# The second batch's keys and queries: transposed by VectorE in 32 by 32 blocks and placed by transfers

## The chip, the cores and the metric

The kernel runs on one core of a Trainium2 chip. The core has five engines with an instruction stream each: TensorE (PE in the profile; its weight loads are PEld), VectorE (DVE), ScalarE (ACT), GpSimd (POOL) and SyncE (SP), which here only issues transfers. TensorE writes to eight banks of PSUM; everything else lies in SBUF, in 128 partitions. The metric is the device time of one execution in microseconds (us), as the median of several runs. Beside it, one execution was recorded by the hardware profiler; all durations of single instructions come from that one.

## What is computed

Windowed attention with a few global tokens, and behind it a two-layer network on all its outputs. There are 8 batches and 8 heads, 512 local and 32 global tokens, head size 64; the model width is 512 and the hidden width 2048. Everything is in 32-bit floats.

```python
scale = 1.0 / np.sqrt(D)
k_all = np.concatenate([k_g, k_l], axis=2)
v_all = np.concatenate([v_g, v_l], axis=2)
out_g = np.matmul(sm(scale * np.matmul(q_g, k_all.transpose(0, 1, 3, 2))), v_all)
s_ll = scale * np.matmul(q_l, k_l.transpose(0, 1, 3, 2))
mask = np.abs(pos[:, None] - pos[None, :]) <= window          # window = 32
s_ll = np.where(mask, s_ll, -1000000000.0)
s_lg = scale * np.matmul(q_l, k_g.transpose(0, 1, 3, 2))
out_l = np.matmul(sm(np.concatenate([s_lg, s_ll], axis=-1)), v_all)
attn_out = np.concatenate([out_g, out_l], axis=2)
x = attn_out.transpose(0, 2, 1, 3).reshape(B * S, H * D)      # 4352 rows of 512
h = x @ w_in
y = (h - np.tanh(h)) @ w_out
```

`sm` is the softmax. The scores of one local token against local keys matter only within 32 places on either side, so a tile of 128 queries needs 192 local keys and the 32 global ones.

## The kernel before

**Tiling.** A head's 512 local tokens are four tiles of 128. Both factors of a score, queries and keys, must lie with the head size of 64 in the partitions. In memory they lie with the tokens outermost, so each head's keys and queries have to be transposed. The keys are then laid out in a buffer of four windows of 224 columns (192 local keys, 32 global ones, line 417 and following).

**Three ways of the attention.** The first two batches (heads 0 to 15) are worked in plain 32-bit floats and in pairs of heads (class `Pair`, eight pairs, pairs 4 to 7 are the second batch): head 2j lies in partitions 0 to 63, head 2j+1 in 64 to 127. `Pair.add_load` (472) loads both heads' keys and queries with the tokens in partitions; `Pair.add_turn` (484) transposes them by TensorE, four 128 by 128 transposes into one bank for the keys and four into another for the queries (line 493), and copies them from the banks to the key windows `first_kw` and to `first_q` (line 324, called from 499 to 504). The first batch has two sets of buffers in turn. The second batch has one set, the third of `SETS` (262): raw tile `rawkq`, key windows `kw0`, queries `hk0`. Batches 2 to 7 are worked head by head with each factor split in a high and a low part; their keys and queries go another way, `add_transposed` (678): loaded in 32 by 32 blocks, transposed block by block by VectorE (691), split, and moved to their windows by transfers (`Head.add_turn`, 780).

**The rest of a head.** Local scores (617, or 879 and 880) go to banks; VectorE masks them and finds the peak (884), ScalarE takes the exponential (891), VectorE the inverse of the sum (627, or 898), GpSimd scales (904), TensorE transposes the probabilities (972, or 1055 among the products of the head before) and multiplies them with the values (649, 1053). The global queries' scores have lines 526 and 827.

**Feed-forward.** A batch's output of 512 tokens is one chunk. Its 16 steps multiply with a block of `w_in` (1136, or 1162 for the first steps of the first chunk), take `h - tanh(h)` (1144, 1147), split it (324, 1153) and multiply with a block of `w_out` into four banks (1199). Each product is made of three passes of high and low parts. The feed-forward work of one batch is spread between the attention of the next. During the first two batches the weights are loaded too, in 32 pieces (377), and split.

**What sets the order.** Every step is recorded by `add` with an engine (or a choice of engines), an estimated duration, a due time and the buffers that it reads and writes. `Order.run` (109) then walks through all steps and emits, again and again, the one that could start first by these estimates, due times deciding between near equals. So the order on each engine, SP's queue among them, is fixed when the program is built, and each engine works strictly in that order. The due times come from a table of numbers, `CFG` (302). `mode` marks kinds of TensorE work; a switch between kinds is given an estimated cost. Only one tile holds the raw and the transposed blocks of the later batches: `raw1` and `kq` are the two halves of `rawkq` (213).

## Time and profile before

| | before |
|---|---|
| median of 3 runs | 1014.32 us (1011.75 to 1015.07) |
| the profiled execution | 1015.1 us, its span 1013.3 us |
| instructions in it | 18,583 |
| granted TensorE clock, mean | 0.999 |
| moved by transfers | 91.66 MB, 90 GB/s on average |

The span is the stretch from the first to the last recorded instruction; 1.8 us of the execution lie outside it. Busy time is the union of an engine's instructions; matmuls overlap their neighbours, so how long a group holds TensorE is read from one start to the next. A releaser ("<-") names what ended an idle time.

### The profile page before, as it was taken

The numbers are of one execution on the slowest core, as the hardware profiler recorded it, in microseconds if no ns is written. First come the engines' busy times: TensorE is split into PE (matmuls) and PEld (weight loads), VectorE is DVE, ScalarE is ACT, GpSimd is POOL, SyncE is SP. The second block draws the span as 40 slices with busy tenths as digits, with TensorE's granted clock in tenths as the row PEclk, the third lists the DMA queues.
The fourth block names the chain that finished last, engine by engine and source line by source line (L and its number), as shares of the span: only waits on it lengthen the run. The fifth ranks groups of instructions, "written<-read, shape, count | busy, mean of one in ns | idle before, by whom it ended". The sixth has DMA issues, their size and how long they took to land.

```text
span 1013.3 us, 18583 instructions
## 1 busy us (share of the span) xinstructions
PE 991.5 (98%) x5648; PEld 826.4 (82%) x5648; DVE 605.8 (60%) x1826; ACT 669.2 (66%) x1783; POOL 613.5 (61%) x839
## 2 busy tenths in 40 slices
PE   6999999999999999999999999999999999999998
PEld 4677777888888888888888888888887888888897
DVE  6965665787668665777558674777657774111110
ACT  5966666886778766878568775877658775422231
POOL 4665556676767765777567765777657774322221
PEclk9999999999999999999999999999999999999999
DMA  9555454443454333543344432643245330100010
GB/s 233 144 152 162 123 149 111 124 93 81 84 124 98 81 76 80 125 86 85 74 106 111 89 84 52 146 91 85 56 93 129 80 88 15 42 1 1 1 42 21
DMA packets 250819, 91.66 MB, mean 90 GB/s; under 512 B 204640, under 2 KB 238176, under 8 KB 250720
## 3 DMA queue, kind: packets, MB, share of 16 engines
q1 hardware_dynamic: 248928, 89.82, 37.9%
q8 instruction: 45, 0.74, 0.3%
q10 hardware_dynamic: 1792, 0.66, 0.2%
q14 instruction: 54, 0.44, 0.1%
HBM read 49.27 MB, written 8.91 MB: 57 GB/s over the span
## 4 chain that ended last, share of the span: by engine, by line
PE 84%; DVE 5%; ACT 2%; DMA 1%; issue 1%; SPq 1%; POOL 1%; ACTq 0%; DVEq 0%; POOLq 0%
PE bank L1199 34%; PE bank L1136 32%; PE bank L1053 5%; PE bank L1055 4%; PE bank L879 2%; PE bank L880 2%; DVE stats L898 1%; DVE prob L884 1%; DVE pg L839 1%; PE bank L827 1%; PE bank L649 1%; PE bank L972 1%; DVE tlo L989 1%; PE bank L617 1%; DMA wraw<-in_moe_w_in_dram 1%
## 5 line engine op out<-in xcount | busy, mean ns | idle before, releaser
L1199 PE MATMUL bank<-w_out_hi,gates 128*128 128x512 f32 x1088 | 302.1, 395 | 0.2
L1153 POOL TENSOR_TENSOR gates<-t,gates 128x512 fp32r<-128x512 f32 x136 | 175.5, 1290 | 171.5 <-PE bank L1199 124.0
L1199 PEld LDWEIGHTS bank<-w_out_hi,gates 128*128 128x128 f32 x1088 | 198.7, 188 | 42.4 <-POOL gates L1153 2.3
L1147 DVE TENSOR_TENSOR t<-bank,t 128x512 f32<-128x512 f32 x136 | 94.0, 691 | 178.2 <-ACT t L1144 176.3
L1144 ACT ACTIVATE t<-bank 128x512 f32<-128x512 f32 x136 | 81.3, 598 | 127.5 <-PE bank L1136 119.3
L1199 PE MATMUL bank<-w_out_lo,gates 128*128 128x512 f32 x544 | 152.2, 393 | 0.0
L1136 PE MATMUL bank<-x_hi,w_in_hi 128*128 128x512 f32 x496 | 137.5, 399 | 0.0
L904 POOL TENSOR_SCALAR prob<-prob,stats 128x224 f32<-128x224 f32 x240 | 106.4, 459 | 45.4 <-DVE stats L899 14.1
L1136 PE MATMUL bank<-x_lo,w_in_hi 128*128 128x512 f32 x496 | 133.7, 391 | 0.0
L1136 PE MATMUL bank<-x_hi,w_in_lo 128*128 128x512 f32 x496 | 133.6, 391 | 0.0
L324 ACT CAST gates<-t 128x512 fp32r<-128x512 f32 x136 | 84.1, 618 | 58.8 <-PE bank L1199 43.8
L891 ACT ACTIVATE prob<-prob,stats 128x224 f32<-128x224 f32 x240 | 113.3, 474 | 10.2 <-DVE stats L884 8.2
L1199 PEld LDWEIGHTS bank<-w_out_lo,gates 128*128 128x128 f32 x544 | 100.8, 188 | 20.1
L884 DVE CUSTOM_DVE_ANT_0 prob<-bank,mask 128x224 f32<-128x224 f32 x240 | 80.9, 388 | 55.4 <-PE bank L880 45.4
L1136 PEld LDWEIGHTS bank<-x_hi,w_in_lo 128*128 128x128 f32 x496 | 91.6, 188 | 19.0 <-issue 0.5
L1136 PEld LDWEIGHTS bank<-x_lo,w_in_hi 128*128 128x128 f32 x496 | 91.2, 188 | 18.2
L324 ACT COPY wraw<-bank 64x288 f32<-64x288 f32 (+1 forms) x130 | 57.8, 446 | 69.8 <-PE bank L1053 48.4
L1136 PEld LDWEIGHTS bank<-x_hi,w_in_hi 128*128 128x128 f32 x496 | 87.9, 189 | 15.0 <-issue 0.2
L1053 PE MATMUL bank<-thi,vv 128*128 128x160 f32 (+2 forms) x384 | 96.8, 294 | 1.6 <-DVE stats L839 1.6
L1055 PE MATMUL bank<-idr,prob 128*128 128x128 f32 x376 | 98.0, 280 | 0.1
L1088 POOL TENSOR_TENSOR x_lo<-wraw,x_hi 64x256 fp32r<-64x256 f32 x96 | 70.6, 735 | 39.7 <-ACT x_hi L324 32.7
L1053 PE MATMUL bank<-tlo,vv 128*64 128x160 f32 (+2 forms) x384 | 89.4, 234 | 0.0
(144 smaller groups left out, 1785.1 us busy)
## 6 DMA issues: line engine op xcount, KB each, us to landing
hl<-hl SPq DMA_DIRECT2D x72, 128.0 KB, 2.3
out_dram<-wraw SPq DMA_DIRECT2D x32, 256.0 KB, 2.4
kw<-hl SPq DMA_DIRECT2D x72, 96.0 KB, 2.2
wraw<-in_moe_w_in_dram SPq DMA_DIRECT2D x12, 512.0 KB, 3.8
rawkq<-in_k_l_dram SPq DMA_DIRECT2D x96, 64.0 KB, 2.3
rawkq<-in_q_l_dram SPq DMA_DIRECT2D x96, 64.0 KB, 2.4
vraw<-in_v_l_dram SPq DMA_DIRECT2D x48, 128.0 KB, 2.4
kw<-hl SPq DMA_DIRECT2D x72, 80.0 KB, 2.1
```

What stands on the lines that cost most here:

```text
L324: (nc.scalar.copy if e == "A" else nc.vector.tensor_copy)(dst, src)
L884: nc.vector.tensor_tensor_reduce(out=self.tile(t)[:, :KC], in0=getattr(self, f"s_{pair}")[:, i, :KC], in1=tile_mask[t], scale=-0.125, scal ...
L891: nc.scalar.activation(x, x, AF.Exp, bias=self.st[:, t:t + 1], scale=-1.0, accum_out=self.st[:, 4 + t:5 + t])
L904: nc.gpsimd.tensor_scalar(x, x, self.st[:, 8 + t:9 + t], 1.0, op0=ALU.mult, op1=ALU.mult)
L1053: nc.tensor.matmul(dst, l, r, start=i == 0, stop=i == len(mm) - 1, skip_group_check=True)
L1055: nc.tensor.transpose(*turns[i // each], idn)
L1088: eng[e].tensor_sub(places()[1], view(total, [(160, 2), (1, P)]), f32(places()[0]))
L1136: nc.tensor.matmul(self.h[s][:, j * n:(j + 1) * n], w[:, cc, f * P:(f + 1) * P], self.x()[xi][:, cc, :n], start=part == 0 and cc == 0 and ...
L1144: nc.scalar.activation(tt_[q], self.h[s], AF.Tanh)
L1147: nc.vector.tensor_sub(tt_[q], self.h.pop(s), tt_[q])
L1153: eng[e].tensor_sub(gg[q][1], tt_[q].rearrange("p (k c) -> p k c", k=4), f32(gg[q][0]))
L1199: nc.tensor.matmul(self.acc[tt], g[:, j * nt + tt], low_out(f) if wi else w_out_hi[:, f], start=s == 0 and k == 1, stop=last and k == 3 * ...
```

## The change

Pairs 4 to 7, the second batch, no longer go through TensorE. For each head, four transfers load keys and queries in blocks of 32 by 32 into `raw1` (128-byte pieces, 512 to a transfer, where a transfer had 512 pieces of 256 bytes before); one VectorE instruction transposes all blocks into `kq`, which puts the keys in partitions 0 to 63 and the queries in 64 to 127; two transfers place the keys in their windows and one the queries. Head 1 of a pair goes the same way through the same tiles after head 0. The scores of a pair now also wait for the second head's keys and queries (`self.more`). The copies of the global keys stay.

The planner changes in three places: the cost of a switch is counted by kinds (plain work to feed-forward cheap, to and from local scores dear; feed-forward steps get `mode=2`), each engine that issues transfers has its own queue in the estimate, and two estimates of first loads are raised. All numbers of `CFG` are new, so all due times are, and the order changes on every engine from the start on.

```diff
+    INTO = 0.03
...
+    @staticmethod
+    def switch(a, b, turn, other):
+        return 0.0 if a == b else turn if a == 1 or b == 1 else other
...
-                        s = max(s, at.get(e, 0.0) + self.XW * max(0.0, o.ldw - tail)) + self.MW * (o.mode != mode)
+                        s = max(s, at.get(e, 0.0) + self.XW * max(0.0, o.ldw - tail)) + self.switch(mode, o.mode, self.MW, self.MV)
...
-                at["Q"] = max(s + 1.1, at.get("Q", 0.0)) + o.xfer
-                done = max(at["Q"], s + d + 0.9) + 1.0
+                at["Q", e] = max(s + 1.1, at.get(("Q", e), 0.0)) + o.xfer
+                done = max(at["Q", e], s + d + 0.9) + 1.0
...
-    CFG = dict(a_g=0.3833, a_gl=1.5118, a_kg=1.3108, a_kq=0.24, a_ph=0.0029, a_qs=9.8856, a_v=2.7859, a_w=0.9693, a_wn=28.6019, a_xg=24.9592,
+    CFG = dict(a_g=0.685, a_gl=11.6239, a_kg=2.2291, a_kq=0.5015, a_ph=0.1338, a_qs=18.5778, a_v=2.1728, a_w=0.1667, a_wn=6.3853, a_xg=18.0447,
...
+            self.blocks = j >= 4
             self.key = SETS[self.set]
+            self.more = [self.key[k] + "b" for k in (2, 4)] if self.blocks else []
...
+        def add_block_load(self, h):
+            srcs = [x[self.b, 2 * self.jj + h].rearrange("(b s) d -> s b d", s=32) for x in (k_l, q_l)]
+
+            def load(e, _):
+                for j, src in enumerate(srcs):
+                    for half in range(2):
+                        p0 = 64 * j + 32 * half
+                        nc.sync.dma_start(raw1[p0:p0 + 32].rearrange("s (b d) -> s b d", d=32), src[:, :, 32 * half:32 * half + 32])
+
+            add(("S", 2.2), load, self.due(self.C["o_ld"] - 8 + h), w=["raw"], xfer=0.9)
+
+        def add_block_turn(self, h):
+            def turn(e, _):
+                nc.vector.transpose(kq, raw1)
+
+            add(("D", 0.69), turn, self.due(self.C["o_ld"] + h), r=["raw"], w=["kq"])
+
         def add_load(self):
+            if self.blocks:
+                self.add_block_load(0)
+                self.add_block_turn(0)
+                self.add_block_load(1)
+                return
+
...
+            def keys(h):
+                def fn(e, _):
+                    r = slice(D * h, D * h + D)
+                    for dst, src in zip(windows(kw[r]), rows(kq[:D])):
+                        nc.sync.dma_start(dst, src)
+                return fn
+
+            def all_queries(h):
+                def fn(e, _):
+                    nc.sync.dma_start(q[D * h:D * h + D].rearrange("p t c -> p (t c)"), kq[D:])
+                return fn
+
+            if self.blocks:
+                add(either(128, "kg"), glob, due, r=["gl0"], w=[pk])
+                for h in range(2):
+                    if h:
+                        self.add_block_turn(1)
+                    add(("S", 1.2), keys(h), due + h, r=["kq"], w=[(pw, self.more[0])[h]], xfer=0.9)
+                    add(("S", 0.6), all_queries(h), due + h, r=["kq"], w=[(pq, self.more[1])[h]], xfer=0.6)
+                return
...
-            add(("T", 1.1), mm, d(0), r=[pw, pk, "gl0"], w=[sg], res=[pgk, plk], alloc=[(sg, self.tag), (sh, self.tag)], tail=0.08)
+            add(("T", 1.1), mm, d(0), r=[pw, pk, "gl0"] + self.more[:1], w=[sg], res=[pgk, plk], alloc=[(sg, self.tag), (sh, self.tag)], tail=0.08)
...
-            reads = self.key[2:]
+            reads = self.key[2:] + self.more
```

What this does to the order is seen at three places. In the rows below, `rawkq` and the tiles with `first_` in their names belong to the first two batches, `wraw` and `first_q` in SP's weight rows are the two landing places of weight pieces. The line numbers of the new kernel are higher by the lines added.

TensorE, between pair 6's parts of the work. Before (the eight rows from the last product of a pair on; L493 are the transposes of pair 6's keys):

```order
L649 MATMUL bank_95<-first_t_86,first_v 64x128
L493 MATMUL bank_96<-idr,rawkq 128x128 x4
L1136 MATMUL bank_98<-x_hi_77,w_in_hi 128x512 x4
L1136 MATMUL bank_98<-x_lo_78,w_in_hi 128x512 x4
L1136 MATMUL bank_98<-x_hi_77,w_in_lo 128x512 x4
L526 MATMUL bank_97<-first_kw_87,first_m 64x512
L527 MATMUL bank_95<-first_kw_87,first_m 64x96
L972 MATMUL bank_96<-idr,prob_92 128x128 x4
```

Now, where pair 6's first local scores stand (L668, behind a product L700 and feed-forward work L1187):

```order
L700 MATMUL bank_97<-first_t_86,first_v 64x160
L1187 MATMUL bank_98<-x_hi_77,w_in_hi 128x512 x4
L1187 MATMUL bank_98<-x_lo_78,w_in_hi 128x512 x4
L1187 MATMUL bank_98<-x_hi_77,w_in_lo 128x512 x4
L668 MATMUL bank_95<-first_kw_87,first_q_82 128x224
L668 MATMUL bank_96<-first_kw_87,first_q_82 128x224
```

No row L493 (L523 in the new kernel) reads `rawkq` any more; the local scores now come straight behind feed-forward work.

SP's queue in the same stage. Before (loads of a pair's raw keys and queries, L476, among weight loads, L377):

```order
L377 DMA wraw_65<-in_moe_w_in_dram 128x4x256
L476 DMA rawkq<-in_q_l_dram 128x4x64 x2
L377 DMA first_q<-in_moe_w_out_dram 128x1024
L377 DMA wraw_65<-in_moe_w_in_dram 128x4x256
L377 DMA first_q<-in_moe_w_out_dram 128x1024
L476 DMA rawkq<-in_k_l_dram 128x4x64 x2
```

Now, pair 6's moves (L542 keys, L547 queries; weight loads are L382):

```order
L382 DMA wraw_65<-in_moe_w_in_dram 128x4x256
L542 DMA first_kw_87<-rawkq 64x2x192
L542 DMA first_kw_87<-rawkq 64x2x160
L382 DMA first_q<-in_moe_w_out_dram 128x1024
L547 DMA first_q_82<-rawkq 64x512
L382 DMA wraw_65<-in_moe_w_in_dram 128x4x256
L542 DMA first_kw_87<-rawkq 64x2x192
L542 DMA first_kw_87<-rawkq 64x2x160
L547 DMA first_q_82<-rawkq 64x512
L486 DMA rawkq<-in_k_l_dram 32x16x32 x2
```

The moves of the two heads stand one behind the other, with two weight loads between them and the next head's raw blocks (L486) behind.

ScalarE at the very start. Before (L388 and L393 handle a weight just landed, the copies of `first_g` bring the global keys to the windows, on which the first scores wait):

```order
L324 ACT_TABLE_LOAD
L324 COPY first_g<-bank_97 128x128
L324 COPY first_m<-bank_97 64x4x32 x2
L388 ACTIVATE wraw_65<-wraw_65 128x512
L324 COPY first_kw<-first_g 128x4x32 x2
L388 ACTIVATE first_q<-first_q 128x512
```

Now:

```order
L393 ACT_TABLE_LOAD
L393 ACTIVATE wraw_65<-wraw_65 128x512
L329 COPY first_g<-bank_96 128x128
L329 COPY first_m<-bank_96 64x4x32 x2
L393 ACTIVATE first_q<-first_q 128x512
L329 CAST w_in_hi<-vraw 128x4x128
L329 COPY first_kw<-first_g 128x4x32 x2
```

The copy to `first_kw` has moved behind a second weight step and a cast; on SP's queue the two weight loads have moved ahead of the values' loads.

More of the change, by code (lines that the diff above doesn't have):

```diff
@@ L152, in run @@
                 s = max(at.get(e, 0.0) + max(0.0, o.ldw - tail), ready_at)
[L153 removed]
+                d = self.tensor_time(s, d + self.switch(mode, o.mode, self.TURN, self.INTO * (o.mode == 2)), o.rows)
                 tail, mode = o.tail, o.mode
@@ L318 @@
     add = order.add
-    order.XW, order.TOL, order.MW, order.KD = CFG["xw"], CFG["tol"], CFG["mw"], CFG["kd"]
+    order.XW, order.TOL, order.MW, order.KD, order.MV = (CFG[k] for k in ("xw", "tol", "mw", "kd", "mv"))
     PEN, PENP = CFG["pen"], CFG["penp"]
@@ L481, in add_load @@
                 add(("S" if self.j or a else "A", 1.1), load(a, (k_l, q_l)[a]), self.due(self.C["o_ld"] - 8) if self.j else -1002 + a,
-                    w=[self.key[a]], xfer=1.46)
+                    w=[self.key[a]], xfer=1.46 if self.j else 2.0)
         def add_turn(self):
@@ L600, in load @@
                     nc.sync.dma_start(first_v[D:D + G, 1, h], bass.AP(g.tensor, g.offset, [[D, G], [0, NT], [1, D]]))
-            add(("S", 2.4), load, self.due(self.C["o_vl"]), w=["vh0", "vh1"], xfer=2.56)
+            add(("S", 2.4), load, self.due(self.C["o_vl"]), w=["vh0", "vh1"], xfer=2.56 if self.j else 3.6)
         def add_local_scores(self, p):
-            reads = self.key[2:]
+            reads = self.key[2:] + self.more
             tiles = (2 * p, 2 * p + 1)
@@ L1170, in add_hidden @@
                 at = due if cc == NCC - 1 else base(2 * cc) + CFG["o_h0"] + CFG["hp"] * s
-                add(("T", 0.69), some(cc), at, r=r, w=[hk], res=[tk] if cc == 0 else (), alloc=[(hk, "acc" if s < 2 else "h")] if cc == 0 else ())
+                add(("T", 0.69), some(cc), at, r=r, w=[hk], res=[tk] if cc == 0 else (), alloc=[(hk, "acc" if s < 2 else "h")] if cc == 0 else (), mode=2)
             for part in range(0 if early else 3):
@@ L1209, in add_out @@
                     g = [(tt, f, wi, gi, f - fs[0]) for f in fs for wi, gi in passes]
-                    add(("T", 0.229 * len(g)), mm(g), due + 0.1 * tt, r=[gk, lk] + wk, w=[accs[tt], ("ord", self.name)])
+                    add(("T", 0.229 * len(g)), mm(g), due + 0.1 * tt, r=[gk, lk] + wk, w=[accs[tt], ("ord", self.name)], mode=2)
             else:
```

25 lines of the change are left out of this document (12 added, 13 removed).

## The prediction

> **What bounds the kernel now.** I read the page first, then the groups of instructions by line, then the table of windows, then TensorE's timeline where the removed work stands.
>
> ```profile
> PE 991.5 (98%) x5648; PEld 826.4 (82%) x5648; DVE 605.8 (60%) x1826; ACT 669.2 (66%) x1783; POOL 613.5 (61%) x839
> PE 84%; DVE 5%; ACT 2%; DMA 1%; issue 1%; SPq 1%; POOL 1%; ACTq 0%; DVEq 0%; POOLq 0%
> 0.00:60.00 60.00, 49.73 (x382) 36.37 (x383) 46.52 (x190) 46.47 (x152) 34.14 (x67) 1.00 0.70 182
> 60.00:175.00 115.00, 113.46 (x647) 88.12 (x646) 72.25 (x184) 75.64 (x183) 68.27 (x72) 1.00 0.50 138
> 175.00:877.00 702.00, 696.01 (x3951) 588.84 (x3950) 467.96 (x1421) 513.06 (x1394) 480.09 (x678) 1.00 0.40 89
> 877.00:1013.30 136.30, 132.29 (x674) 113.06 (x672) 19.12 (x32) 34.03 (x56) 31.05 (x25) 0.99 0.06 19
> ```
>
> The first two rows are the page's engine table and its chain of waits; the others are windows (length; busy time of PE, PEld, DVE, ACT, POOL; granted clock; DMA share; GB/s). TensorE is busy 98% of the span and is 84% of the chain. Its 21.8 us of idle lie at the start (60.00 - 49.73 = 10.3), in the second batch's stage (1.5), in the six later batches (6.0) and at the very end (4.0). So a microsecond of TensorE work taken out from 60 us on should come out of the time, and only 1.5 us of that stage is idle that a better order could win.
>
> **The change part by part.** *1. The transposes taken from TensorE.*
>
> ```profile
> L493 PE MATMUL bank<-idr,rawkq 128*128 128x128 f32 x32 | 4.9, 279 | 1.0 <-ACT first_t L324 1.0
> 98.45 1.07 PE L1199 MATMUL bank<-w_out_hi,gates 128*128 128x512 f32 x4
> 99.36 0.60 PE L493 MATMUL bank<-idr,rawkq 128*128 128x128 f32 x4
> 99.72 1.18 PE L1199 MATMUL bank<-w_out_hi,gates 128*128 128x512 f32 x4
> 100.74 1.08 PE L1199 MATMUL bank<-w_out_lo,gates 128*128 128x512 f32 x4
> ...
> 138.14 1.04 PE L493 MATMUL bank<-idr,rawkq 128*128 128x128 f32 x8
> 139.01 0.60 PE L972 MATMUL bank<-idr,prob 128*128 128x128 f32 x4
> ```
>
> The group row gives 4.9 us for the 32 transposes of the second batch (four pairs of heads, keys and queries, four each), but its durations overlap their neighbours. Starts tell more: four transposes push the next matmul from 99.36 to 99.72, and the four feed-forward matmuls behind them take 1.02 us to the next start (99.72 to 100.74) against 0.91 from 98.45 to 99.36. One group of four so costs 0.36 + 0.11 = 0.47. Where two groups stand together, 138.14 to 139.01 is 0.87, or 0.44 each. Eight groups: 3.5 to 4.9 us; I take 8 x 0.46 = **3.7**. The 1.0 us of idle in front of one group waits for a ScalarE copy that the products behind it may need as well; between 0 and 1.0 I take **0.5**.
>
> *2. Switches.* The new order enters feed-forward work 212 times instead of 222 (counted in both orders).
>
> ```profile
> 391.92 1.17 PE L1136 MATMUL bank<-x_hi,w_in_hi 128*128 128x512 f32 x4
> 392.93 1.07 PE L1136 MATMUL bank<-x_lo,w_in_hi 128*128 128x512 f32 x4
> 393.83 1.07 PE L1136 MATMUL bank<-x_hi,w_in_lo 128*128 128x512 f32 x4
> ...
> 372.30 0.35 PE L879 MATMUL bank<-kw,hl 128*128 128x224 f32 x1
> 372.49 0.27 PE L880 MATMUL bank<-kw,hl 128*128 128x224 f32 x1
> 372.60 0.28 PE L879 MATMUL bank<-kw,hl 128*128 128x224 f32 x1
> ```
>
> The row at 391.92 follows a product, as the one at 372.30 does: there the first four feed-forward matmuls take 1.01 us against 0.90 for the next four, 0.11 per entry. Ten of them would be 1.1 us. But the entries that vanish mostly become products followed by scores (26 instead of 12), and there the first score takes 0.19 against 0.11, so most of the price only moves. Between 0 and 1.1 I take **0.3**.
>
> *3. VectorE, the queue and the memory path.*
>
> ```profile
> L324 DVE COPY first_kw<-bank 128x384 f32<-128x384 f32 (+1 forms) x16 | 7.6, 513 | 4.0 <-PE bank L493 4.0
> L324 DVE COPY first_q<-bank 128x512 f32<-128x512 f32 x8 | 5.4, 679 | 0.0
> L691 DVE STREAM_TRANSPOSE rawkq<-rawkq x54: 445/711/714, 143.5 to 818.5; 128x512 f32<-128x512 f32 x48, 128x256 f32<-128x256 f32 x6
> 144.97 0.91 SPq L687 DMA_DIRECT2D rawkq<-in_k_l_dram  x2
> 145.93 1.02 SPq L687 DMA_DIRECT2D rawkq<-in_q_l_dram  x2
> 170.15 1.25 SPq L792 DMA_DIRECT2D kw<-hi  x2
> 175.13 0.49 SPq L797 DMA_DIRECT2D hi<-hi  x1
> q1 hardware_dynamic: 248928, 89.82, 37.9%
> kw<-hl SPq DMA_DIRECT2D x72, 96.0 KB, 2.2
> hl<-hl SPq DMA_DIRECT2D x72, 128.0 KB, 2.3
> ```
>
> VectorE loses the bank copies of four pairs (half of 7.6 + 5.4 is 6.5 us) and gains eight block transposes of 0.71 (5.7 us): 0.8 us less, on an engine busy 72 of 115 us. The per-head steps are those that the later batches already run, so their rows are the prices: a head issues four loads (0.91 + 1.02), two key moves (1.25) and one query move (0.49), 3.7 us of SP's time, 29 us for eight heads, less some 8 for the loads removed. Each head moves about 1,340 more pieces (2,048 + 320 instead of 1,024); a packet costs 0.379 x 1013.3 x 16 / 248,928 = 25 ns of one engine, so eight heads add 10,750 x 25 / 16 = 17 us of the 16 engines together, and the DMA share of the 115 us stage goes from 0.50 to about 0.64. All this lies beside TensorE's feed-forward work. I cost it at **0**, if the moved keys come in time.
>
> Whether they do is a chain: the move of head 0's keys waits until the previous pair's last local scores have read the single key buffer; the query move follows; then VectorE may overwrite the one transposed tile with head 1; then its moves. In issue and landing that is 1.25 for keys, 0.34 for a weight load that the queue now holds between (row below), 0.49 for the query, 2.3 to land, 0.71 for the transpose, and again 0.34, 1.25, 0.49 and 2.3: **9.5 us**.
>
> ```profile
> 134.15 1.20 PE L649 MATMUL bank<-first_t,first_v 128*64 128x160 f32 x16
> 135.28 1.20 PE L1136 MATMUL bank<-x_hi,w_in_hi 128*128 128x512 f32 x4
> 102.64 0.34 SPq L377 DMA_DIRECT2D first_q<-in_moe_w_out_dram  x1
> SPq L377 <- DVE wraw L397: 25.2, 10, 6.5
> ```
>
> The cover is what the order puts on TensorE between a pair's last local scores and the next pair's first. From pair 5 to pair 6 (pairs 4 to 7 are the second batch) it is ten groups of four feed-forward matmuls (9.1 us), two groups of products (1.13 each, 134.15 to 135.28) and eight transposes (0.9): 12.3 us. From 4 to 5 and 6 to 7 it is over 17. The margin is 2.8 us at the tightest place, so 0; bound 0 to +9.
>
> *4. The start.* The diff sets all due times anew, so the first microseconds change too.
>
> ```profile
> 1.78 2.77 SPq L588 DMA_DIRECT2D first_v<-in_v_l_dram  x3
> 5.72 0.43 SPq L377 DMA_DIRECT2D wraw<-in_moe_w_in_dram  x1
> 10.10 0.68 ACT L388 ACTIVATE wraw<-wraw 128x512 f32<-128x512 f32 x1 [1.95 <-DMA wraw<-in_moe_w_in_dram]
> 10.68 0.48 ACT L324 COPY first_kw<-first_g 128x128 f32<-128x128 f32 x2
> 11.21 3.36 PE L617 MATMUL bank<-first_kw,first_q 64*128 64x224 f32 x16 [3.79 <-ACT first_kw L324]
> ```
>
> The first scores wait 3.79 us for a ScalarE copy that stands in line behind a weight still on its way (issued at 5.72, there at 10.10). In the new order that weight and the next are issued where the values stand now (1.78), but ScalarE handles both, and a cast, before the copy. With the same 4.4 us on the way the copy could end near 9.3 instead of 11.2. Against it, VectorE too handles the first weight before the first keys, global scores now go ahead of the local ones, and 1 MB of weights shares the way with the first keys. Bounds -1.9 and +1.5 (the two kinds of weight load below differ by that in landing, 5.3 against 3.8); I take **-0.5**, since VectorE and ScalarE pace that stage.
>
> ```profile
> wraw<-in_moe_w_in_dram SPq DMA_DIRECT2D x12, 512.0 KB, 3.8
> first_q<-in_moe_w_in_dram SPq DMA_DIRECT2D x4, 512.0 KB, 5.3
> ```
>
> *5. The six later batches.* Same work, new order. 6.0 us of idle can be won at most; a new order may as well double it. I take 0, bounds -6.0 and +6.0. In the last 136 us the two orders read alike: 0.
>
> **Sum**: -3.7 - 0.5 - 0.3 + 0 - 0.5 + 0 = **-5.0 us**. The profiled execution took 1015.1 us (span 1013.3 and 1.8 around it), so it would become 1010.1. It lies 0.8 above the median of 1014.3, and the median is what I forecast: **1009.3**.
>
> **Rivals.** *A: the gain is given back early.* Eight of the 32 transposes (pair 4) stand before 25 us, where VectorE and ScalarE pace the work; and the start may be 1.5 later. Then -6 x 0.46 - 0.3 + 1.5 = -1.6, or 1012.7. For it: only 49.7 of the first 60 us are busy on TensorE. Against: the first scores begin at 11.21, and 49.7 us of work find room in that stage only if TensorE is nearly full from there on.
>
> *B: the new order also closes gaps of the later batches.* Two thirds of 6.0 gone: 1009.3 - 4.0 = 1005.3. For it: such a gap needs only one late chain moved. Against: the works between scores, transposes and products are as far apart on TensorE as before (about 3 us at the shortest in both orders).
>
> *C: slower, by the moved keys.* In the queue's new order two weight loads stand among pair 6's moves and three among pair 7's. In the trace such a load has waited up to 6.5 us for its buffer, and SP works in order, so everything behind waits with it: the moves, then the transpose on VectorE, behind that the subtraction for the next gates, and last TensorE's local scores. Two waits of 6.5 make pair 6's chain 22.5 us against 12.3 of cover: a stall of 10.2 and 1009.3 + 10.2 = 1019.5. It decides from about 2.8 us of waits on, and makes the kernel slower beyond doubt from 8 us of stall. For it: the single buffers for raw, transposed and placed keys. Against: those waits sum to only 25.2 us over ten loads.
>
> [...]
>
> **How the numbers follow.** What a measurement here can tell from no change is about 0.3%, or 3 us. Forecast (gain of 3 to 8 us): 0.45. A (within 3 us): 0.27. B (more than 8): 0.13. C (slower by over 3): 0.15. So faster 0.58, same 0.27, slower 0.15. The range leaves out most of C and half of B: **1003 to 1018**; the forecast's own is 1006 to 1011.
>
> **What would show it.** Right: TensorE's busy time about 4 us lower; no idle over 0.5 us in front of the local scores (L668 of the new kernel) after 60 us; the window from 175 to 877 of its length within 2 us; first local scores near 10 to 11 us. A shows as a later end of the first 60 us' work, B as a shorter stretch of the six batches, C as waits of the local scores for key transfers, with the queue waiting on weight buffers. I am wrong if the later batches change by more than the transposes do.

## The result, and the profile after

The changed kernel takes 1024.97 us (median of 5 runs, 1022.95 to 1026.26), the kernel before 1014.32 in the same comparison: a ratio of 1.011, with a 95% interval of 1.0091 to 1.0128. It is slower by 10.6 us; I had forecast 5.0 less. The profiled execution has a span of 1022.9 us, 9.6 more than before.

The engine table and the chain of the page, and the same four windows as in the prediction (length; busy time of PE, PEld, DVE, ACT, POOL; granted clock; DMA share; GB/s), of the changed kernel:

```profile
PE 991.1 (97%) x5616; PEld 822.5 (80%) x5616; DVE 618.1 (60%) x1865; ACT 659.2 (64%) x1736; POOL 618.6 (60%) x843
PE 82%; DVE 5%; DMA 4%; ACT 3%; issue 2%; POOL 2%; SPq 1%; ACTq 0%; DVEq 0%; POOLq 0%
...
0.00:60.00 60.00, 47.84 (x350) 33.66 (x350) 46.24 (x192) 46.30 (x144) 35.30 (x65) 1.00 0.77 188
60.00:175.00 115.00, 113.36 (x640) 87.09 (x641) 68.71 (x196) 74.96 (x174) 69.33 (x74) 1.00 0.60 159
175.00:877.00 702.00, 688.19 (x3905) 581.03 (x3905) 483.45 (x1450) 500.15 (x1355) 476.66 (x672) 1.00 0.40 88
877.00:1022.90 145.90, 141.68 (x723) 120.68 (x721) 19.75 (x30) 37.73 (x66) 37.30 (x34) 1.00 0.05 19
```

The 32 transposes are gone (5616 matmuls instead of 5648), and yet TensorE is idle for 31.8 us instead of 21.8. The third window shows where: 13.8 us idle in the six later batches against 6.0, in a stage whose work the change does not touch. The first window has lost 1.9 us more; the second, in which most of the moved work lies, is as full as it was.

A second reading uses the feed-forward matmuls as milestones, since both kernels do as many of them (3,360 in the trace) in nearly one sequence. On TensorE's timeline, the n-th of them starts later than before by

| n-th feed-forward matmul | 1 | 400 (183 us) | 600 | 800 | 1600 | 3200 |
|---|---|---|---|---|---|---|
| changed kernel, us | +1.2 | +1.3 | +6.2 | +6.3 | +9.7 | +9.4 |

So 1.2 us are lost before the first of them, and from there to the 400th, where most of the second batch is worked, the two kernels come out even: the gain that I had forecast is not there. 5.0 us are lost where the third batch begins, 3.4 more between the 800th and the 1600th, and on balance none behind that. The waits of TensorE between 170 and 900 us (releaser: us in total, times, longest), first before, then after (L879 is now L930, L827 is L878, L1053 is L1104, L1055 is L1106):

```profile
PE bank L879 <- DVE tlo L989: 2.6, 3, 1.5
PE bank L1053 <- DVE stats L839: 1.6, 5, 0.3
PE bank L827 <- DMA kw<-hl: 0.6, 1, 0.6
```

```profile
PE bank L930 <- DMA hl<-hl: 5.4, 6, 1.6
PE bank L930 <- issue: 2.0, 2, 1.8
PE bank L930 <- DVE tlo L1040: 1.7, 3, 0.8
PE bank L1106 <- DVE stats L890: 1.2, 5, 0.3
PE bank L878 <- DMA kw<-hl: 1.0, 1, 1.0
```

The new waits are those of a later head's local scores (L930) for the moves of its queries (`hl<-hl`). One place where much is lost at once, on SP's queue and on TensorE in the changed kernel:

```profile
184.81 3.61 SPq L843 DMA_DIRECT2D kw<-hl  x4
188.46 1.19 SPq L738 DMA_DIRECT2D rawkq<-in_k_l_dram  x2
189.70 1.02 SPq L738 DMA_DIRECT2D rawkq<-in_q_l_dram  x2
190.81 1.13 SPq L848 DMA_DIRECT2D hl<-hl  x2
...
190.24 0.41 PE L878 MATMUL bank<-kw,qgt 128*128 128x384 f32 x1 [0.98 <-DMA kw<-hl]
193.93 0.34 PE L930 MATMUL bank<-kw,hl 128*128 128x224 f32 x1 [1.55 <-DMA hl<-hl]
```

The two query moves of this head are issued behind the four raw loads of the next one (2.2 us of issue), and the scores wait for them. Before, the same stretch reads:

```profile
179.43 3.47 SPq L792 DMA_DIRECT2D kw<-hl  x4
183.00 0.57 SPq L797 DMA_DIRECT2D hl<-hl  x1
188.89 0.34 PE L879 MATMUL bank<-kw,hl 128*128 128x224 f32 x1
```

The key moves of this head start at 179.43 instead of 184.81, one query move stands ahead of the raw loads and one behind them (185.95), and the scores wait for nothing. So the raw loads are not all of it: the key moves were late already. In the changed kernel SP's queue stood still for 3.4 us in front of them, waiting for ScalarE to make their input `hl`. ScalarE makes it ahead of a tile's exponentials before, and behind four of them and further casts now; the first row is of the kernel before, the second of the changed one:

```profile
178.36 0.61 ACT L324 CAST hl<-rawkq 128x512 fp32r<-128x512 f32 x1
184.18 0.61 ACT L329 CAST hl<-rawkq 128x512 fp32r<-128x512 f32 x1
```

The start, on TensorE and ScalarE of the changed kernel:

```profile
8.94 0.66 PE L446 MATMUL bank<-idr,wraw 64*128 64x64 f32 x4 [3.17 <-DMA wraw<-in_q_g_dram]
12.79 2.93 PE L668 MATMUL bank<-first_kw,first_q 64*128 64x224 f32 x16
...
8.17 0.70 ACT L393 ACTIVATE wraw<-wraw 128x512 f32<-128x512 f32 x1 [3.96 <-DMA wraw<-in_moe_w_in_dram]
11.43 0.49 ACT L329 COPY first_kw<-first_g 128x128 f32<-128x128 f32 x2
```

The first weight, issued at 1.79 now, is there at 8.17, after 6.4 us instead of 4.4. The global queries, issued by ScalarE's queue at 2.42 as before, let their transposes start at 8.94 instead of 6.73. The first local scores come at 12.79 instead of 11.21.

### The profile page after: what moved, and what is told of

The parts are those of the page before. It is cut to its first block, busy times and chain, and to the rows that moved or that the text cites. A ratio compares the mean times of both kernels' runs of the same rounds, so it can differ in the third digit from the quotient of the medians.

```text
span 1022.9 us, 18618 instructions
## 1 busy us (share of the span) xinstructions
PE 991.1 (97%) x5616; PEld 822.5 (80%) x5616; DVE 618.1 (60%) x1865; ACT 659.2 (64%) x1736; POOL 618.6 (60%) x843
## 4 chain that ended last, share of the span: by engine, by line
PE 82%; DVE 5%; DMA 4%; ACT 3%; issue 2%; POOL 2%; SPq 1%; ACTq 0%; DVEq 0%; POOLq 0%
PE bank L1250 32%; PE bank L1187 30%; PE bank L1104 5%; PE bank L1106 4%; PE bank L930 2%; PE bank L931 2%; PE bank L668 1%; PE bank L700 1%; DMA hl<-hl 1%; ACT prob L942 1%; PE bank L1023 1%; DMA out_dram<-wraw 1%; DVE pg L890 1%; PE bank L577 1%; DVE stats L949 1%
## 5 line engine op out<-in xcount | busy, mean ns | idle before, releaser
L1187 PE MATMUL bank<-x_hi,w_in_hi 128*128 128x512 f32 x496 | 135.6, 395 | 0.0
L1187 PE MATMUL bank<-x_hi,w_in_lo 128*128 128x512 f32 x496 | 134.8, 394 | 0.0
L1187 PE MATMUL bank<-x_lo,w_in_hi 128*128 128x512 f32 x496 | 134.1, 392 | 0.0
L1187 PEld LDWEIGHTS bank<-x_lo,w_in_hi 128*128 128x128 f32 x496 | 91.4, 188 | 18.5 <-issue 0.2
L1187 PEld LDWEIGHTS bank<-x_hi,w_in_lo 128*128 128x128 f32 x496 | 91.2, 188 | 18.1 <-issue 0.3
L1187 PEld LDWEIGHTS bank<-x_hi,w_in_hi 128*128 128x128 f32 x496 | 89.3, 189 | 16.4 <-issue 0.5
L1106 PE MATMUL bank<-idr,prob 128*128 128x128 f32 x376 | 98.1, 280 | 1.8 <-DVE stats L890 1.2
L1104 PE MATMUL bank<-thi,vv 128*128 128x160 f32 (+2 forms) x384 | 96.9, 294 | 0.7 <-DVE stats L890 0.4
L1104 PE MATMUL bank<-tlo,vv 128*64 128x160 f32 (+2 forms) x384 | 89.4, 234 | 0.0
L1104 PEld LDWEIGHTS bank<-thi,vv 96*128 96x128 f32 (+1 forms) x384 | 75.1, 196 | 6.6 <-POOL prob L955 2.7
```

The lines of the kernel that those rows point to most:

```text
L1104: nc.tensor.matmul(dst, l, r, start=i == 0, stop=i == len(mm) - 1, skip_group_check=True)
L1106: nc.tensor.transpose(*turns[i // each], idn)
L1187: nc.tensor.matmul(self.h[s][:, j * n:(j + 1) * n], w[:, cc, f * P:(f + 1) * P], self.x()[xi][:, cc, :n], start=part == 0 and cc == 0 and ...
```

## The experiments

All ratios are to the kernel before, from the same chip and job, with 95% intervals; the changed kernel stands at 1.011 (1.0091 to 1.0128). Kernels that keep an order "word for word" emit it from a written list of operations with engine and bank, in place of the planner. Lines in the rows of such kernels are shifted; the operation is named where it matters.

### 1. The loads behind the query moves

```diff
  SP's queue, one later head, as the list of its operations
  key moves x4
- raw loads of the next head x4
  query moves x2
+ raw loads of the next head x4
  output stores x3
```

> The changed kernel with one edit: on SP's queue each later head's raw loads are put behind the query moves that follow them (41 heads); every other engine's order is word for word that of the changed kernel. Theory Q (the later batches lose because small moves that scores wait for stand behind big loads): the waits of L930 for hl (5.4 us in the changed kernel) go, the 702 us window of the later batches gets 5 us shorter, time 1024.97 - 5.4 = about 1019.6 (1018 to 1021). Rival L (the whole chain of a head is late in the new order, the loads are only what is seen last): the wait moves to another name, time 1023.5 to 1026; with loads 1.2 us later it may even get 1 to 2 us worse.

Measured: 1026.62 us, ratio 1.0118 (1.0099 to 1.0136): nothing gained. The waits that theory Q names did go, and others came (L1156 is the products, L1302 the second feed-forward product):

```profile
PE bank L1156 <- POOL prob L1007: 6.0, 5, 1.8
PE bank L1302 <- ACT wraw L381: 2.2, 2, 2.0
```

The rows at one end of a batch show how, on SP, on ScalarE and on TensorE:

```profile
416.74 2.18 SPq L900 DMA_DIRECT2D hl<-hl  x2
419.02 1.11 SPq L790 DMA_DIRECT2D rawkq<-in_k_l_dram  x2
420.18 2.23 SPq L790 DMA_DIRECT2D rawkq<-in_q_l_dram  x2
422.45 3.18 SPq L1332 DMA_DIRECT2D out_dram<-wraw  x3
...
424.69 0.59 ACT L381 COPY wraw<-bank 128x512 f32<-128x512 f32 x1 [2.69 <-DMA out_dram<-wraw]
...
429.27 0.31 PE L1156 MATMUL bank<-thi,vv 128*128 128x160 f32 x1 [1.80 <-POOL prob L1007]
```

The output stores are now behind the loads (in the changed kernel they go out at 418.48). ScalarE waits 2.69 us for the store's buffer, all its exponentials stand behind that copy, GpSimd normalizes late, and TensorE waits 1.80 us for probabilities. The loads were what TensorE's wait pointed at, not what it hung on. The idle time of the later batches went from 13.8 to 12.8 us (702 less 689.21), and part of the rest went by another way: behind two of the new waits (1.5 us that ended at 546.1, 1.2 us that ended at 665.0) the granted clock fell to 0.50 for 3.4 us each, which is 1.7 us of TensorE's work each time (an estimate: half of 3.4). The clock over the whole execution is 0.991 to 0.995 in the five executions of this kernel, and 0.997 to 1.0 in those of the changed kernel.

### 2. The stores ahead of the loads as well

```diff
  SP's queue, one later head
  key moves x4
- raw loads of the next head x4
  query moves x2
  output stores x3
+ raw loads of the next head x4
```

> The changed kernel with the raw loads of the later heads put behind the query moves and behind the output stores that follow them (41 query moves, 19 stores); other engines as they were. With the loads only behind the query moves, the stores went out 4 us later, ScalarE waited for the store's buffer and TensorE for probabilities. Theory H (SP's hand-over at the ends of the batches is the bottleneck, and what stands last there is the loads that nobody waits for soon): both kinds of wait shrink, 1024.97 - 5 = about 1020. Rival (the loads are then waited for themselves, or the queue is full there whatever its order): 1024 to 1028.

Measured: 1026.85 us, ratio 1.014 (1.0114 to 1.0167). The rival holds: the waits of the scores for query moves fall to 0.5 us, but two groups of waits for normalized probabilities add up to 10.7:

```profile
PE bank L1211 <- POOL prob L1062: 7.2, 5, 2.0
PE bank L1213 <- POOL prob L1062: 3.5, 1, 3.5
PE bank L1037 <- DMA hl<-hl: 0.5, 1, 0.5
```

### 3. The first two weights later

```diff
  SP:       first queries
-           weight 0, weight 1
            first values
+           weight 0, weight 1
  ScalarE:  [weight 0,] store of global keys, [weight 1,] copies of global keys
+           [weight 0, weight 1 behind these copies]
  VectorE:  [weight 0,] first keys, [weight 1,] first queries
+           [weight 0, weight 1 behind these]
```

> The changed kernel with one edit at the start: the first two weight loads go behind the first values on SP's queue (where they were before the change), and ScalarE's and VectorE's steps on them behind the copies that the first scores need; everything from 15 us on keeps its order. Theory S (the start loses because two loads of 512 KB were put ahead): the global transposes start near 6.7 instead of 8.94, the first local scores near 10 instead of 12.79, time 1024.97 - 2.5 = about 1022.5. Rival (the work of that stage is only put elsewhere, VectorE and ScalarE pace it anyway): first scores earlier, but the feed-forward work starts no earlier than 69 us and the time stays at 1024.5 to 1025.5.

Measured: 1026.08 us, ratio 1.0112 (1.0095 to 1.0129): no faster. The stage itself did what theory S says, as TensorE's timeline shows (L490 transposes the globals, L712 are local scores):

```profile
6.12 0.66 PE L490 MATMUL bank<-idr,wraw 64*128 64x64 f32 x4 [0.40 <-DMA wraw<-in_q_g_dram]
9.97 2.33 PE L712 MATMUL bank<-first_kw,first_q 64*128 64x224 f32 x16
...
14.00:16.00 2.00, 0.24 (x3) 0.00 (x1) 2.00 (x13) 2.00 (x9) 0.96 (x1) 1.00 1.16 233
18.00:20.00 2.00, 2.00 (x10) 1.77 (x9) 1.50 (x6) 1.91 (x6) 2.00 (x5) 0.50 1.22 298
```

The scores start 2.8 us earlier than in the changed kernel. Then TensorE runs into VectorE's maxima (VectorE is busy 2.00 of 2.00 us at 14 to 16), stands nearly still for 2 us, and its clock is granted at 0.50 from 18 to 20 us. The first feed-forward matmul is 0.7 us earlier, the 400th 0.9, and the later batches take that back: their idle time is 16.9 us now (702 less 685.06), although their order is that of the changed kernel. (The profiled execution is the slowest of four, 1.8 us above their median.)

The same lever was tried in the kernel before, where a copy of global keys waits in line behind a weight:

```diff
  ScalarE:  store of global keys
-           weight 0, copies of global keys, weight 1
+           copies of global keys, first exponential, weight 0, second exponential, weight 1
  VectorE:  first keys, first queries
-           weight 0, weight 1, four maxima
+           two maxima, weight 0 and two maxima in turn, weight 1
```

> The kernel before with one edit at the start: the two copies of global keys on ScalarE, which the first scores wait for (3.8 us), go ahead of the first weight's step, and VectorE's first four maxima go ahead of its weight steps (7 and 8 places move). Theory S (the first microseconds are set by weight steps that stand ahead of the scores' inputs): first scores at 8.9 instead of 11.2, feed-forward work starts up to 2 us earlier, 1012.3 to 1013.5. Rival (VectorE and ScalarE pace that stage, the wait only moves on): 1014 to 1015.

Measured: 1015.2 us, ratio 1.0018 (1.0006 to 1.003), which is what the rival said. The first scores start at 8.80 instead of 11.21, and the first feed-forward matmul starts 2.0 us later than before: again a gap (2.19 us in front of the second global scores) and a lower clock behind it.

```profile
8.80 3.36 PE L775 MATMUL bank<-first_kw,first_q 64*128 64x224 f32 x16 [1.29 <-ACT first_kw L436]
17.73 1.67 PE L684 MATMUL bank<-first_kw,first_m 128*64 128x512 f32 x2 [2.19 <-DVE first_kw L436]
...
16.00:18.00 2.00, 0.27 (x1) 0.19 (x2) 1.93 (x7) 1.43 (x6) 1.66 (x4) 1.00 0.94 217
18.00:20.00 2.00, 2.00 (x6) 0.81 (x5) 1.50 (x6) 0.82 (x2) 2.00 (x6) 0.52 0.96 323
```

### 4. The path without the table, and the table without the path

In both kernels the planner orders the work anew.

```diff
-            self.blocks = j >= 4
+            self.blocks = False
```

> The new table and the planner's new rules, but the second batch's keys and queries stay on TensorE (blocks off); the planner orders this work anew. Theory T (the transposes' path is worth its 3.7 us, the table makes the loss): 1024.97 + 3.7 = about 1028.7, at least 1021. Theory P (the path by blocks and moves makes the loss, the table is harmless): 1012 to 1016. The planner's order differs from both known ones, so 3 us either way are open.

```diff
-    CFG = dict(a_g=0.685, a_gl=11.6239, ...
+    CFG = dict(a_g=0.3833, a_gl=1.5118, ...
...
-    INTO = 0.03
+    INTO = 0.0
...
-                at["Q", e] = max(s + 1.1, at.get(("Q", e), 0.0)) + o.xfer
+                at["Q"] = max(s + 1.1, at.get("Q", 0.0)) + o.xfer
...
```

> The old table and the planner's old rules, with the second batch's keys and queries by blocks and moves; the planner orders this work anew. Theory T: 1014.3 - 3.7 = about 1010.6, at most 1014. Theory P: 1020 to 1025. The planner's order differs from both known ones, so 3 us either way are open.

Measured: new table with the transposes on TensorE, 1027.34 us, ratio 1.0124 (1.0106 to 1.0142); old table with the new path, 1024.58 us, ratio 1.0095 (1.0077 to 1.0112). The first agrees with theory T (the table makes the loss, the path is worth a little), the second contradicts it; theory P is met in the second and contradicted by the first. Both are slower by about 1%, whatever was kept. That neither half of the change keeps the old time was the first sign that the order itself, and not what it is made for, decides.

### 5. One part of the order exchanged

```diff
     def run(self):
-        ready = [o for o in self.ops if o.n == 0]
...
+        for x in ROWS.split():
+            n = next(i for i, c in enumerate(x) if c.isalpha())
+            o, e = self.ops[int(x[:n])], x[n]
+            o.args = {tok: int(j) for (tok, _), j in zip(o.alloc, x[n + 1:])}
+            o.fn(e, o.args)
```

ROWS holds the operations planned up to the seam in the one kernel's order, and all others in the other's.

> The changed kernel's work and its order word for word up to the place planned at 158 us (a little ahead of the first later head's global scores); behind it every engine's order is that of the kernel before, word for word. Theory O (the loss lies in the new order of the later batches, wherever its waits show): idle of TensorE from 175 to 877 us back to about 5 to 6 us, time 1024.97 - 8 = about 1017 (1015 to 1019). Rival E (the early part leaves the later batches late or starved whatever order follows, since weights, gates or head 16's tiles come late): 1021 to 1026, with the waits of the first heads at 184 to 231 us still there.

> The mirror: the kernel before (second batch on TensorE) in its own order up to the place planned at 164 us, and behind it the changed kernel's order, word for word. Theory O: 1014.3 + 8 = about 1022 (1020 to 1024), with 12 to 13 us of idle on TensorE from 175 to 877 us. Rival E: at most 1017.

Measured: new then old 1020.15 us, ratio 1.0055 (1.0041 to 1.0069); old then new 1028.17 us, ratio 1.0138 (1.0117 to 1.0159). The window of the later batches, first of new then old, then of old then new:

```profile
175.00:877.00 702.00, 694.52 (x3944) 588.09 (x3944) 466.08 (x1421) 512.43 (x1393) 480.82 (x677) 1.00 0.41 89
```

```profile
175.00:877.00 702.00, 686.38 (x3893) 580.77 (x3894) 480.60 (x1448) 498.50 (x1350) 473.51 (x669) 1.00 0.40 89
```

Theory O holds in its main point. With the old order behind the seam, the later batches are idle for 7.5 us, with the new one for 15.6, whichever part stands ahead; and from the 400th to the 3200th feed-forward matmul new then old loses only 0.3 us, as against 7.4 in old then new and 8.2 in the changed kernel. But both times lie above its ranges. New then old is 3 us slower than the 1017 expected: the early part with the change in it does not gain, it loses (its 400th feed-forward matmul comes 4.1 us late). And the two parts together (5.9 and 13.9 us) come to more than the whole, so a seam probably costs something by itself: in old then new one wait of 3.7 us for key moves stands at the seam.

### 6. One engine's order exchanged

```diff
  SP's queue of the kernel before, one later head (45 query moves in all)
  key moves x4
+ raw loads of the next head x4
  values x3
  query moves x2
- raw loads of the next head x4
```

> The kernel before with one edit on SP's queue: 45 query moves of the later heads get the raw loads of the next head put ahead of them (the order that I blamed), all other engines' orders word for word. Theory Q (the place of the loads in the queue is what costs): 1014.3 + 4 to 10 us, with waits of L879's successor for hl. Rival D (distance: in the old order the scores stand far enough behind the moves, so the queue's order costs nothing there; in the new order they stand too close): within 2 us of 1014.3.

Measured: 1037.66 us, ratio 1.0228 (1.0207 to 1.0249), with these waits in the later batches:

```profile
PE bank L1037 <- DMA hl<-hl: 16.8, 15, 2.8
PE bank L1037 <- DVE tlo L1147: 4.0, 5, 1.5
```

Theory D falls, and Q's half that experiment 1 could not show holds, at more than twice the 10 us that I had allowed: the loads ahead of the query moves cost 23 us over 45 moves, about half a microsecond each. The old order has no slack in that place; it has the loads where they do no harm.

> The changed kernel, with SP's queue behind 158 us in the order of the kernel before, word for word (56 places differ); TensorE, VectorE, ScalarE and GpSimd keep the new order. Theory Q' (in the later batches the new order loses through SP's queue alone): 1024.97 - 8 = about 1017 (1015 to 1020). Theory C (it loses through the compute engines' order, and each order needs the queue it was planned with): 1023 or more, possibly slower than the changed kernel.

> The mirror: the kernel before, with SP's queue behind 164 us in the changed kernel's order; all other engines keep the old order. Theory Q': 1014.3 + 8 = about 1022. Theory C: within 2 us of 1014.3, since only 56 places differ and the scores of the old order stand where they stood.

Here SP's queue alone is in the other kernel's order behind the seam of experiment 5 (56 places differ). Measured: changed kernel with the old queue 1041.46 us, ratio 1.0268 (1.0245 to 1.0291); kernel before with the new queue 1031.69 us, ratio 1.018 (1.0164 to 1.0196). The first is as theory C says and excludes Q'. In the second C's number is wrong by far, and Q' is nearer: 56 exchanged places cost the old order 18 us. In both exchanges the queue fits only the order that it was planned with.

```diff
  TensorE, changed kernel, at 57 places of the later heads
- local scores of a head
  feed-forward matmuls x4
+ local scores of a head
```

> The changed kernel with one edit on TensorE: 57 groups of local scores of the later heads change places with the group of four feed-forward matmuls behind them, so that they come 0.91 us later; all other engines as they were. Theory D (in the new order the scores stand too close behind the moves they wait for): the 7 us of waits of the scores mostly go, 1024.97 - 4 = about 1021. Rival (every step behind the scores is then 0.9 us later and the waits come back there, at the transposes of the probabilities and the products): 1025 to 1035.

Measured: 1039.38 us, ratio 1.0251 (1.0232 to 1.027). The rival holds: the scores' waits for query moves are gone from the list, and other steps wait: global scores (L986) for VectorE's sums, transposes (L1213) for normalized probabilities, the feed-forward work (L1357) for a copy on ScalarE. From the 400th to the 3200th feed-forward matmul this kernel takes 12.4 us more than the changed one; 6.6 of them are idle time of TensorE, and in the other 5.8 the matmuls themselves take longer from start to start (global scores 6.5 more, local ones 3.4 less).

```profile
PE bank L986 <- DVE wraw L1240: 4.8, 10, 0.8
PE bank L1213 <- POOL prob L1062: 4.0, 6, 1.0
PE bank L1357 <- ACT wraw L436: 2.6, 2, 2.2
```

From the end of a head's last query move on SP to its first scores, the median of 48 heads is 2.69 us before and 2.35 in the changed kernel, and the shortest are 1.85 and 1.79. Both orders run at the shortest distance in many places, the new one in more. But this experiment shows that distance there is not to be had for nothing: the steps behind are as close.

### 7. Other orders of the unchanged work

```diff
- d_y=49.9741, ... s_wl=29.0213, step=15.4752, step1=18.4221,
+ d_y=49.9741, ... s_wl=29.0213, step=16.0, step1=18.4221,
```

> The kernel before with one number of its table changed (step 15.4752 to 16.0, a distance between due times of the later batches); transposes stay on TensorE, the planner orders anew from about 255 us on. Theory M (the old order is a rare one, in which the waits happen to close; nearly any other order of the same work loses 5 us or more): 1020 to 1030. Theory N (the loss belongs to the new table and its order): 1012 to 1017.

```diff
- hs=5.7779, lag=10.5363, last=0.0,
+ hs=5.7779, lag=13.0, last=0.0,
```

> A second sample of the same kind: the kernel before with lag 10.5363 changed to 13.0 (when the feed-forward work of a batch is due); the order changes from about 270 us on. Theory M: 1020 to 1030. Theory N: 1012 to 1017.

Measured: 1030.91 us, ratio 1.0161 (1.0142 to 1.0181), and 1031.17 us, ratio 1.0174 (1.0157 to 1.0191). Theory M holds in both, at about 1 us above its range. Up to the 600th feed-forward matmul they stand within 1.0 us of the kernel before; behind it they lose 16 and 13 us, with 16 us of listed idle from 175 to 877 us instead of 5.1. No transpose was moved in them. With the changed kernel and the two of experiment 4 these are five orders planned anew, and all five are slower by 1.0 to 1.7%.

### 8. The path in the order of before

```diff
-            self.blocks = j >= 4
+            self.blocks = j in (5, 7)
```

All other work is in the order before, word for word; the block loads, block transposes and moves of pairs 5 and 7 are put in where their inputs allow.

> The kernel before in its own order, word for word, but with the keys and queries of pairs 5 and 7 by blocks and moves (these two have 13 to 16 us on TensorE between the last local scores of the pair ahead and their own first scores; pair 6 has 5.5 us and stays on TensorE, as pair 4 does). Theory T (the path itself is worth 0.46 us for each group of four transposes): 16 transposes gone, 1014.3 - 1.8 = about 1012.5 (1011 to 1014). Theory P (the path by blocks and moves costs by itself, through queue, tiles or memory path): 1016 or more, with waits for moved keys, or VectorE and SP late behind them.

> As old_two_pairs (the order before, pairs 5 and 7 by blocks and moves), but pair 5's block loads and first transpose stand at 53 to 61 us of the plan, behind the values, where they were at 21 to 33. Theory T: the first 60 us are as before, and four groups of transposes less make 1013.5 - 1.8 = about 1011.7 (1010.5 to 1013). Theory Z (whatever TensorE saves there is waited for again at the later batches' hand-overs): 1013.5 to 1015.5.

> The same with pair 5 alone by blocks and moves. Theory T: 1013.5 - 0.9 = about 1012.6. Theory Z: 1013.5 to 1014.5.

Measured: two pairs 1015.17 us, ratio 1.001 (1.0 to 1.002); with the loads later 1014.63 us, ratio 1.0009 (1.0 to 1.0019); one pair 1013.73 us, ratio 1.0007 (0.9998 to 1.0015). Theory T's gains of 1.8 and 0.9 us do not appear, and theory P's loss does not either. The window from 60 to 175 us shows why, here of two pairs with later loads:

```profile
60.00:175.00 115.00, 111.97 (x626) 85.71 (x624) 69.62 (x180) 73.84 (x179) 64.95 (x71) 1.00 0.56 149
```

TensorE has less to do there, and it is idle for 3.0 us in place of 1.5 (2.6 with one pair). By the milestones, from the first to the 400th feed-forward matmul, the transposes save 0.9 us with one pair and 1.8 with two, and idle time rises by 1.4 and by 2.0 to 3.2, so that this stretch becomes 1.6 to 3.0 us longer; the later batches, whose order is unchanged, then come out 0.9 to 2.6 shorter, for which no cause is shown. (The two profiled executions with two pairs lie 2.2 and 2.7 us above their medians, that with one pair on its median.) So what the transposes leave is waited away in the same stage, and theory Z is what remains for the times.

> The changed kernel's second batch, with both other parts put back: the first two weights behind the first values at the start, and from 158 us on the order of the kernel before. Theory T (the path by blocks is worth 3.7 us of TensorE, once order and start are as before): 1011 to 1013. Theory Z (the path gives back what it saves inside the first 175 us, in idle time in front of probabilities' transposes and global scores): 1015 to 1019.

This kernel joins the edits of experiment 3 (changed kernel) and the first one of experiment 5. Measured: 1019.2 us, ratio 1.0056 (1.0042 to 1.0069). Theory Z again, at the upper end of its range. Its 400th feed-forward matmul is 2.1 us late. At the start it has the clock at 0.63, 0.50, 0.50 and 0.66 in the four windows of 2 us from 16 to 24, and TensorE waits 5.1 us in all for VectorE's maxima and for probabilities before 175 us. I found no version that beats the kernel before.

## Why the prediction was wrong, step by step

**Step 5, the six later batches, failed, and with it the sum.** I took 0 and bounds of -6.0 and +6.0, on the ground that it is the same work. It was +8.2 us, by the milestones from the 400th to the 3200th feed-forward matmul, beyond my bound; 7.9 of them are idle time of TensorE, and the matmuls themselves took 0.3 us more. The bound was an invention: that idle time "may as well double" came from no row. Experiment 7 gives the price that the step lacked: two other orders of the unchanged work cost 16 and 18 us by their ratios. I had counted in the new order that products are followed by scores 26 times instead of 12, and priced this as a switch; what it means for the steps that wait was not priced. "I am wrong if the later batches change by more than the transposes do" is what happened.

**Step 1, the transposes, was right and its gain did not stay.** Up to the third batch's first scores, the keys' and queries' transposes take 9.0 us of TensorE from start to start before and 5.3 after: -3.7. The 1.0 us of idle in front of one group is gone too. But in the same stretch global scores cost 1.3 us more (they now run first, where they take longer: 1.94 us for two at 10.60 against 1.07 for two at 17.11 before), the probabilities' transposes 1.0 more, the products 0.4 more, and idle time rises by 2.2 in all. Rival A, that the gain is given back early, was right in kind for this part; it still left a gain of 1.6 where there was a loss of 1.3 at the 400th feed-forward matmul, and its 1012.7 lacked the later batches. The switches (step 2, 0.3) cannot be told apart from this.

**Step 3, VectorE, the queue and the memory path, held for the wait that it costed.** No local score of the second batch waits for a moved key in the changed kernel; the DMA share went to 0.60 (I had 0.64); VectorE is at 60% as before. So rival C's mechanism did not occur: that the time was slower, as C had it, came another way, by the order of the later batches. That the path costs nothing else is not shown: in experiment 8 the stage that has it lost 1.6 to 3.0 us.

**Step 4, the start, had the wrong sign.** I took -0.5, from a weight that would again be 4.4 us on the way. It took 6.4, and the transposes of the global queries beside it started at 8.94 us (6.12 in experiment 3, where the weights go later). The first feed-forward matmul came 1.2 us later, inside the bound of +1.5 in this execution; in the five experiments that share this start (1, 2, 5, 6 twice) it came 1.4 to 3.9 later, and the 400th 0.7 to 6.0 later. So the even result of the early part in the changed kernel's one profiled execution is among the better ones. Experiment 3 shows that undoing it starts the stage earlier (first scores at 9.97 us instead of 12.79) and brings no time (1026.08 us).

**What stays open.** That most of the loss in the profiled execution lies in the order from the third batch's start on is shown (experiment 5), as is that none of the places tried in it carries the loss alone: the loads' and the stores' place in SP's queue and the scores' place were each changed, and the wait came back one step further on (1, 2, 6). No experiment moved the cast of `hl` on ScalarE by itself, which stands 5.8 us later in the new order at the third batch's start. Why the old order closes nearly all these waits, and which property a planner would have to look for, I could not show. Nor is it known how the table of before was found: if it is the best of many that were tried, any new order is likely to be slower, and five slower ones say little more than that. Pairs 4 and 6 were never moved in the old order. So it stays open whether the path by blocks would win in an order as good as the old one.

## What to carry to other kernels

In a kernel like this one, at 98% of its bound engine and with an order written by a planner, a change that makes the order anew is first of all a draw of a new order: cost it by what another draw costs (here 1.0 to 1.7%, five of five slower), and then add the part that was meant. A wait in the profile names what came last, not what to move: test it by moving it, and read who waits next. To try such a change, keep the old order word for word and exchange only the operations concerned; the answer here for two of the four pairs, no gain, was then clear within 0.1%.

## What the runs showed of the hardware

The clock in the first 60 us. In the first windows the profile's clock reads 1.00, but the traces of the kernels before and after hold no record of the clock before 15.1 and 15.2 us, and there matmuls take nearly twice as long as later (two of 512 columns 1.94 us at 10.60 in the changed kernel and 1.07 at 18.30). After a gap of about 2 us (TensorE busy for 0.24 of 2 us at 14 to 16 us in experiment 3, 0.27 at 16 to 18 in the kernel before with earlier copies) the windows of 2 us behind it show a granted clock of 0.99, 0.50 and 0.66 in the first and of 0.52 and 0.63 in the second, and 1.00 after; taken as time at 0.50 and time at 1.00, that is 3.4 us at half clock. In both, the first scores came earlier, by 2.8 and 2.4 us; at the first feed-forward matmul 0.7 us of that were left in the one, and the other was 2.0 us late.

The same happens later. Six kernels share the order of the first 130 us, and each has a gap of 1.5 us near 39 us. In four of them the clock then falls to 0.50 for 3.4 us, in two (the changed kernel among them) it does not. In the rows below (as the windows above), 40 matmuls fall into four microseconds of the changed kernel behind that gap, and 20 into the same four of new then old; the third row is the first of the two places in experiment 1:

```profile
42.00:46.00 4.00, 4.00 (x40) 3.01 (x37) 3.30 (x14) 4.00 (x14) 3.10 (x5) 1.00 1.09 244
42.00:46.00 4.00, 4.00 (x20) 2.90 (x22) 2.31 (x12) 3.61 (x12) 3.59 (x6) 0.59 1.11 278
547.65:551.06 3.41, 3.41 (x11) 2.76 (x10) 2.58 (x8) 2.61 (x6) 2.74 (x3) 0.50 0.74 189
```

By an estimate, half of the 3.4 us at 0.50, the wait of 1.5 us so cost TensorE 1.7 us more than its own length in those four. In the profiled executions of the kernels before and after, the clock does not fall between 60 and 1010 us, so between these two it is no part of the loss. From 175 to 877 us it falls in nine kernels of the experiments (1, 2, 4 with the new table, 5 old then new, 6 three times, 7 twice), for 3.4 to 10.2 us in all (the granted clock of these nine executions is 0.993 to 0.998 on average), so part of what those lost is this.

In the first 60 us gaps of 1.5 to 2.2 us stood ahead of a fall of the clock, and in experiment 1 waits of 1.5 and 1.2 us did later on. With the same gap of 1.5 us it fell in four executions and not in two, and no run shows what decides. The fall cannot be all of the 2.6 us by which these six differ at the first feed-forward matmul: with the fall it comes 1.4 to 3.9 us later than before, without it 1.2 and 2.2.

SP's queue. Half a microsecond per move is what a load of two times 128 KB in front of a query move cost here (experiment 6, 23 us over 45 moves), although SP issues for only 388 of the 702 us of the later batches in that kernel. 16.8 of the 23 us are seen as 15 waits of scores for query moves: its price lay at the few places where somebody waits for the queue's end.
